# Attention and gated Fourier mixing on one core: keys of one more batch transposed on TensorE, inverse factors loaded from ScalarE's queue, split first loads and last inverse, new order

## The chip, the core and the metric

The kernel runs on one core of a Trainium2 chip. TensorE (PE) multiplies matrices from SBUF into PSUM, VectorE (DVE), ScalarE (ACT) and GpSimd (POOL) work element by element, and 16 DMA engines move data for the queues of SyncE (SP), ACT and POOL. The metric is device time in microseconds (us); a comparison takes the median over several runs.

## The reference

Eight batches, eight heads, 576 positions, head dimension 64, 32 packed queries `p` per head. The output has 576 x 512 values of float32 per batch.

```python
def sm_attn(qq, kk, vv):                 # softmax(scale * q k^T) v
    ...
p_packed = sm_attn(p, k, v)              # 32 packed rows per head
out = sm_attn(q, p_packed, p_packed)     # every position looks at the packed rows
x = out with heads side by side          # 576 x 512
proj = x @ w_proj                        # 576 x 1536
x1, x2, x3 = three parts of proj
x2_conv = irfft(rfft(x2) * rfft(filter_fft))     # along the 576 positions
y = x1 * x2_conv * x3
return y @ w_out
```

## The kernel before

Each batch passes four stages, which the source writes as generators and interleaves over neighbouring batches (`together`, line 1088): `front(b)` does both attentions, `turn(b)` the projection and the forward transform, `middle(b)` the product with the filter's spectrum and the gates x1 * x3, `back(b)` the inverse transform and the output projection.

*Loads.* `load(b)` (line 622) brings k, v and q of a batch as tiles kn, vn, qn (float32 in memory, float16 in SBUF) through POOL's queue, two buffers each. Lines 638 to 654 start the filter, the forward factors wc and wt, the weights wp in three parts, the inverse factors ac (line 652, POOL's queue, four planes of 576 columns: three factors, and a fourth plane that holds negated values of the first two) and wout. POOL's queue has up to eight loads under way; the next one waits for a landing.

*front(b).* The keys are needed with head dimension on the partitions. `k_turn(g)` (line 729) transposes two heads on PE, six products of 96 columns into PSUM (tile kTp), copied to SBUF (tile kT, a ring of five) by DVE or ACT in turn; four such groups make a batch. For the batches in `KEYS` (line 606: 6 and 7) four DMA transposes on SP's queue do it (line 770). `q_turn` (line 750) does the same for q, or one DMA transpose per batch for those in `TURNED`. Then come `score1` (tile s_b), the exponential e, the product with v (pv), its division (rz, ppn), a transpose into ppk, the second scores `score2` (s_b, s2t_b), their exponentials, sums zs, reciprocals zr and the normalised weights a2n.

*turn(b).* Products qp with wp, copied to qm by ACT; products fp and fpt with the forward factors, copied by ACT (ez, fa) and combined (fa); a2n transposed to a2t, on PE or, in batches 5 to 7 (`FLIP`), by one DMA transpose on SP's queue.

*middle(b).* `spectrum(m)` makes f on PE, DVE multiplies it with the filter (tt; the tile h3 or "h" is the filter's spectrum, made at the start from the products hp), POOL adds (gm). `gate` makes x1 and x3 on PE (shown as x_b), ACT copies x1 (x1s), DVE multiplies (w).

*back(b).* `inverse(m)` (line 1033) multiplies gm with ac, for one block m of 128 channels over the first 512 columns: for batches other than 0 three products over 288 columns (even positions) and three over 224. Batch 0 (`APART`) uses another set of five products and is the only one that reads ac's fourth plane. DVE multiplies the result with w into y. A last call covers the remaining 64 columns of all four blocks (into yt). `project_out(n)` (line 1048) multiplies 128 columns of y of all four blocks with wout (tile o_b), copies to os and stores. For the last batch it works in two halves of 256 columns, one copied by ACT and one by DVE; the last call (n = 4) stores each half by itself, half the rows from SP's queue and half from ACT's.

*Order.* The generators don't set the final order. A recorder (class `Recorder`, line 221; in the profile all its instructions have line 538) notes every operation, and a planner (`schedule`, line 316) walks through time with costs for each operation and queue. Among the operations that are ready on an engine it takes the one with the lowest number in a table `PRIORITY` written into the source (line 86, a packed string with one entry for each operation). The instructions go out in that order, each engine's own. Where PE would have nothing in the first 34 us, the planner inserts filler products on zeros ("spin", lines 382 and 1129).

Of the kernel before, what the change touches and what calls it, by code (L numbers as in the profile page):

```python
# [19 lines left out]
P = 128  # L20
# [23 lines left out]
def _constants(S):  # L44
# [37 lines left out]
    ac = _f16(np.stack([*inv, np.where(COLUMN_T % 2 == 0, -inv[1], -inv[0])]).transpose(1, 0, 2))  # L82
# [4 lines left out]
    'c-oy-2RxN+8$ZuEMoLCSBqSoqmKCxq$1Ege%gPMN-Xmm0_RP)}iYVE#3W<sc8S$z&Q8?%MoPE&y`@Z+Po-^*}y6@}0{@1*3f587`q5+rudu2{1'  # L87
    '8~O8>?SK{W-z*%YoO~+%Tt%^qQ}W9U2RlaHGHLgJl$x5MTjnE|O=tXmbA`*LWsEs{+0(W2u5F=3<VZLF^xH>q4MinR3hA+#L$2=GUWVuNsrK=('
    'P?H64>q|+UKWnSXPlIHbwCnrUz3>H84Ekhorn#g_O|LykA@SxMO{a^7*i8=VRcVk5*jOEYF{Kve?CYLpb+yu2k?}gE`7^}VDcHP&v97D5g`1Jl'
    'HEm@FTSaqAEn`Dfc?Ctdq@<PvTu??*l}}Av@dCfvWmOFsEir*WO#@9axr_5UHlexow*(;f!h!>W+@!#fy-Gg%<0>f!!z{!}=7*d=(+Z4h(%UJo'  # L90
    '1TNEt^!E4kcSm<u29r?H{vsVCg}{_5XU9kHd;8=)3!dKd?TsHpO;mJ}-=kiV2Qlrj5)3!lHcNDm(BJka+r#_m*3fK8M)K@??|{Z9D#BE3G|<R>'
    '%%f|w91psiJ1H~9PFyxYn(CGmXt+7v&Gqx>Dy=VbwfWc=InKss!X#>GYohugqqXPdGFxMBRX;a3Gl{e?Z8syMtXl<>Xm#&#2iaA{KIB?iN&P}Y'
    '2B>YGW3OY{__V93Vf1IqY;D!E)|y|nl^r#GovrhgS=o(Eh2M%d8^0D8RW`jIO!)phCg(|AW{22}s`#DS53W<u&si4!Iy`LJ5<WnAejrF@;^)ET'
    'Z^x+)uJkW`9-gCsY_!NhzW)-8W^ftkQC5@sfym|ASN_RbM5ShAVCc;Tm4qCeRa$A|Qlulh5u4U23ukAtysU!svdrAH+*)KQWzA~!JioZMu!Sv;'
    'xrPPbpikFy!MpL%=h^M$)P_YlR!OFa^w5I9+Jvszg{Go`+2QwUoy(VKtWMbkSO(f8I)vE?Ojgw~Oi)p4ULc)*9r;DIac1`E(pXBAi=YCx)SOmG'
    'VysK>QUTr65Z&gF<!WvP0T#8j10&UoZ9fB2$djY{Y8qaa2-;09NlL$G`t(%sOO<rv<445^_mP1IHtMm#ul^bdoA%%k);%k|k4&DCU0jV_L4aFa'
    '_88Mqj#C0Bj*5#Mq2}j2%5(Z83zhKxgF<vHM-H7v0_^NG^ibwwl)zDFX*UJu!5;6dCF^7s1LN_%dTZ*+qAAx*`6vrRr8hDM!@|n>Ha?OMjZl+w'
    'P``zOXVv{#J}(Y#-lqP1{cCNQl@@(_jH$f2M*~ld*vAO}g!o%RXJ^LWjP?%q4ZrGZ>1*z4?s}nn?*#Y8rgCCl*2kZo9HPfs%7$vX>kZxsEN&W&'
    'Q?j0*=KR6c_;jSTx!_CGapO;RX*a5Frq~tU4+j9)*c$(yv!d;^)U=>%b65dW&h&Goj<nzk{<VGUo8D~$&CeevL8Cn?e4RaXzb8c&+`3_SQ%KX_'
    'wYIf8ZUTl_Kx!^MnH`w@{B3by#PEv4>>g6n&~RUmxZBsSy109}`iC0F_yt(`>gan$7}(r0Ft}@B?eDJPA*XNcaL32T-PXzN7mb^-tg5NlxpaXB'  # L100
    'dq-;@E0e=sj>?@S$#ta%>f4jD((=6DnQY`}`yCKZyzNuusV>39-jrKxP*T+QxY(gF!a6U*qqO>#T>mA<dvHBd7Dakt87a6P$FRPQ<29G6yEK`}'
    'hdXnt>-s;o-Eg?yDyA!GB%;f&$KcH9$ml|EIXUtG;w^RSteVG#R5^AoeFuK|3r6O9^+j)97IL?WjRKt{FH;|&<Dg)BtpJyiInTFr$5=n&Q966+'
    '^zT%aIn_zJ*Wy#UG0!R{2HJflD4iZh<;IXPbuw#D$w22MoNb;ewsg<bl$OJJM8nd(UaJdhsziuANDI&7FayeqUe>>k>S!6u;Nsa&i~O?w8TQxU'
    '%%_2tbcxFd7&Q!B|3yK~%*{YWx%W7X`Y87y%Bj<&fA1HeAZJ{lUt-+9J~lr|GR=GdgwpTRhp5ShU*g}G<X`MQl3%jfnpd@v?^jh8pYXco5?hfD'
    'MO<dEUHRsd)~LW_lhW|;3VV@R0n0a4x#cfXJL=k>S2nsO6qi?~*EbYBRF{0(o!4Urx6{&q-@X;<;cLvqB0y`Q=X+iHE~%MiW@MasSM}4xzs|=~'
    '96GjdfL3(Au47=bYpnmX#*gyO{4=RVVTlgPretd?C8R~0*@!YkBwxBj)R{Pb#8o*rJ`vV+VKVKDkpWPxpFg<fp`<IU@0qA*znfirXr)=G827lS'
    'xNXv#oBN`M^tCW4N!=@Y1xb3Ie$Jbr%Pt?>R(!hqMn`Mj&knXCm)2Gw$s0D7ju}c(9}oUMZxmoTT;I~wQW2KZ)jseo#6pw@M#5?;4-W~n_?>JY'
    'a63NBD99)EO=^8(_>B7~-|>}&!P%MOg1oaz%Emfeib`@9^$aB>IYgMX*{+*i(L5!~by-M8#++S6LHU5XxPU6>6}n3|s8#suLm4=ILNtbc3PI^t'
    'PZq|#7z+5AU*xG{yc`-*QyKK|FLEKz6tUy{ha|Zq5Bmir#7D`_P9?4lri84B-Vdutj7<=BDe$^y?W$tTMMkT3-A&d^!v9_jh3YY*JMo`%wN>QV'
    'IXh)!4>_OUmXV+zT72?_YV7xq!#XdXv=-FLBRgaN=7-4Ixmx=~O-ZM=oS5VBk&TnOz^fyhELC(VO5Y)KSW|5Cllmgd+SP_@!ptm3g-(}7D|xf$'  # L110
    'r$)^Kqsg9|qsz)yB`kQkR3qWyE;fTT=|780U#&E=(I~Rn#rv-Zw)W2Ve*Vz)PFVAC{bH|ILF!H8t4tzK!b&sB%3ZUA?1Q4cGD<4rQtt$Y=al;8'
    'hZyQ7+o;+{)kJs)KhAE*4twx2`bI|T{i)|QJu8d-tL=3HhiSjCE2tPbR`ELcTKmcB>#N@Kf@@o<b(s233r2psU)DeQYsDZ$0HFU4BVAyiI{B*J'
    '$lhvI>^Sot9&s}Z-76h#H_4#6f!6U!eK)Q&)#k(XjCn6=$nQU8c+S`RQPr85^)|;nE&-uoRpHr2QNC4t2jM0i6ZP&d?w`|Pd2cRoTFB;nTjB7i'
    '-@>Cb$2PaXr`egE6Q2Xsyw54a*#&1h7wP*|V~@q~q(}v~D>o?RD%J?{aOqSf?R!aitjI~?9{J)pIpX^(=2GZ7E2K<PK*B)P(py<w%g|F?%It=P'
    'wSl#nx=yFdg3Kx-D{X38ep_w$!jWHOqhu7DX%we*nAl#jOrEJ#?jTc<vk!dm1}<`NZEs6NbaX^?N@7e<erAwYV_E*A`*kfrg-?s@{i^H}no{Bu'
    '{gT})b9_^?eV;$ePs;PGr=-ZQdh!C%zlUwVpbDP`%PBblH99Rdg>ylU?Uj$;zb;a+S2C1V(lLX3I@!KmBlpSip1V6S`{KjNM-g>y8JcI5_d;vC'
    ')**9Ig=w+Rvbx?3_A&G~jz1a-`c~po7!@q>ab|vEkY-`A;=H1atelIZm1k4Ivu6XHZ{M~ilAg+$q^DtB-FHQtU6A`c&-{KVjbCDxfn75V!+p=v'
    '`nn4TD?+-PU$gw~%qnj$INIJ6?&DTu;U5zbnwwSERv6WCg|Sr=k&y00Q{3C07t>na&{$AkU7l-KsaO%5<J9#rH{0A)(BtNfu%Vv*rir&bjbF>F'
    'R(>O$DdKIjlB!>(KlaY8;lF2_<C1WrBD%uMNI?700TK9Q`QVc_zU7*M>l+pM*)avNArWh1+}}si?<Kldmj>T@R#N$Jo#LY2#Q>MPUVM39S2C#S'
    'n%}JXe@Ly1%`Se(?*2QGcWz?pZfr!0_KBRb%-ICNW{=yR8h#=tC||VlpE<Qx=E`yN9t(S+OrNdPiYO4Hk$}q~=*0G1fO;9*<m45uN<ZW{;6iJf'  # L120
    'rWJ5E2*Kx}AH#cIL&F3vmTh67u6)ldDNg<EVz{BTYl@oX8*5Gnb;X!m87Fs*e0M!l&zBn^7o_4G+23}LaF?x9@vHCU)VUw+<>NQ)VM{{)MT%+i'
    'oNx%Q6H~ZHYP?HpaG0AL!=1vAiT#HJuJf8qomJ#lP~l!ee5XZ%i^K7{{<obyv*2n95;oo0z4Cm=IrIgOt4Uj!*;#ve+1;tls7LfxR}I_gM*EMn'
    'J87I)F@HZc`ghMt=f?Qlhriny)wp#jNZWpqpFk#?NT2bx<)+><vqTGgEFYw$qhy(-InB$#dyM1vxubI?u(zH=<F4<f-esI*@0|a&F}YgYmT-i#'
    'mHH_u4J$J%{bA~yl2hM$XNTABF3o^s>CPWIx=3ar>%bC;N5dF^A}ACJKmiP)Mo<*N&|DG#^$$VKKmZ740r~|kffM@Q2#VbVf+hgK?usD@VI69U'
    'n6Pu0A^5KeC5QS&4{-8ZHlp<acqV!Qh+ai3iD3~T!pZ<d*szA-yn&k`5Qt_10EonFhL!?}O~g3}>s<h^2|I%uV7MsRZ9YQ&OTyX&U_c=OjG-99'
    '=)y2iYe3W(l?13a6c4&(#&+Oat6*D+g0d4uM2bMv4^e0#1P4LD9Z@C@HenNt>mWqVA(jS+!~r}Y^bm%MAc#f}*+Y)A7m61kgqWP17zpBjpiQDN'
    '6oJ}>jGUYdpS{E|K_mhJqN0sahMvVJBw)vf8^BcGme}SFLT!maZ31pH0|d6!2i7qF6bB9yND%KZkSKF7J8iGE9YMjM#Hhs=6cXHp?!OU$ts#8H'
    '5rPL`9e{Eah}aGX*a>L|I=s;U674lyBK*O5P~!C3k#P_t1lP)N^+db^iFt@ZitZqoet}sEC2AOuKczJ;HAzT_S*SGHg10-lHnD?E^!z4{g;9n}'
    'CX`0hejv7SZ9NF&4)vrYs1*c){s|q3SxN9INMMs-_#mMxg6Q@SC3NwPjg58mgC+ENg6nZ0s?gBl0EE!lfIpZ1)(3&aJODuCQli`jcS-+)w^0Ox'
    '5d%m3OTujl;u8-BLs^fhClG?%6>r!U5jSJ#wv&VyBWfL?yl`oS`{HB(C~SAGZ_9rW@()cEyCFf2ki9sy0HHkoZU5WurX7bZN(q9Phi)1O$ktf^'  # L130
    '!k|bbF1bK-6W(6i=!8K#2nym_CgIS9U@jxO)M2I|m|nlNWY-k{z#sk)e63*r&}9kYgNzFT1pGrU#G^r?njpbGOqQXYw~2WGfY2?G$p6=+f6z_v'
    'D83xgurYX`03I0X@P+IM0*--y!DZ3*2x9XF%SU3qyKY_pwizIiyRTdz{<Z~y{OLZnt&?t7jl&1oUWUY$BXP@jqXIx&euIC|4Z+O<#0~&3_ZrCd'
    'n*m64Y7%!J92VpbgE4$0^3SFbEdlYJgUE0Ye?D(Ri%m-+Wf0<<Dc1G><WCTHvxV&N6J%F#@NdL6qqB%m$~ypqf6|Jnd~AVj(SHDhSUi3'
# [3 lines left out]
class Op:  # L137
# [43 lines left out]
    def hold(self):  # L181

        if self.engine == "POOL":
            return 780
        return 1000 + 0.45 * self.packets() if self.what == "dma_start_transpose" else 440
# [7 lines left out]
    def transfer_ns(self):  # L193

        far = self.ins[0] if self.reads == [] else self.out
        piece, size = far.shape[-1] * mybir.dt.size(far.dtype), far.size() * mybir.dt.size(far.dtype)
        self.piece_ns = max(piece / 25.2, 16) if piece > 1000 or self.engine == "POOL" else max(piece / 21.5, 17)
        if self.reads and self.engine != "POOL" and piece > 1000:
            self.piece_ns = piece / 18
        if self.what == "dma_start_transpose":  # L200
            piece, size, self.piece_ns = 256, self.out.size() * 2, 20
        return size / piece * self.piece_ns / 16
# [18 lines left out]
class Recorder:  # L221
# [3 lines left out]
    SLOW = 6000.0  # L225
# [90 lines left out]
    def schedule(self):  # L316
# [18 lines left out]
        def live():  # L335

            heads = [q[0] for q in queues.values() if q]
            beside = 31 if len(heads) > 1 else 0
            total = sum(max(x[1].piece_ns, beside if x[1].what == "dma_start_transpose" else 0) for x in heads) * (1.6 if moved[0] < self.SLOW else 1.0)
            return [(x, x[1].piece_ns / total) for x in heads]  # L340
# [82 lines left out]
        def issue(e, t):  # L423
            while free[e] <= t + 1e-6:
# [19 lines left out]
                if op.dma():  # L444
                    took = op.hold()
                    begins = t + (2760 if e == "POOL" else 950)
                    opens[e] = max(opens.get(e, 5900 if e == "POOL" else 0), begins)
# [43 lines left out]
        while events:  # L491
# [20 lines left out]
            elif what == "moved" and x == turn[0]:  # L512
                advance(t)
                for e, q in queues.items():
                    if q and q[0][0] <= 0.02:
                        op = q.pop(0)[1]
                        at(t + (1500 if e == "POOL" else 600), "done", op)
# [27 lines left out]
def kernel(  # L545
# [23 lines left out]
    NI = ac_np.shape[1]  # L569
# [19 lines left out]
    ac = const.tile([P, NI, S], FP16, tag="ac", name="ac")  # L589
# [16 lines left out]
    TURNED, KEYS, NK = (4, 5, 6, 7), (6, 7), 5  # L606
# [562 lines left out]
```

## Time and profile before

| what | value |
|---|---|
| median of 5 runs | 189.47 us (188.94 to 196.76) |
| the profiled execution | 189.87 us |
| its span in the profile | 188.1 us |
| DVE, ACT, POOL busy | 143.1, 123.5, 137.6 us |
| landings of kn, vn, qn of batch 0 | 12.46, 15.29, 17.95 us |
| landings of wp's three parts | 22.26, 24.43, 27.16 us |
| landings of kn, vn, qn of batch 1 | 30.18, 33.42, 36.16 us |
| ac: issued, landed, first used | 24.71, 38.30, 38.81 us |
| last product on PE ends | 182.8 us |
| last store lands | 186.73 us |

Times are counted from the start of the span. An engine's busy time is the union of its instructions; a product on PE is counted from its start to its modelled end, and products overlap, so the distance between two starts is what one costs. The granted clock of PE was 0.99 of full over the span. Loads are counted in bytes written.

### The profile page before, as it was taken

How to read it: one execution, taken by the hardware profiler on the slowest of the kernel's cores; microseconds unless marked ns; L12 is line 12 of the kernel's file. 1: busy time of each engine (PE TensorE's matmuls, PEld its weight loads, DVE VectorE, ACT ScalarE, POOL GpSimd, SP SyncE). 2: the span in 40 equal slices, each digit the busy share in tenths (PEclk: the TensorE clock that was granted, in tenths of full speed). 3: DMA queues.
4: the chain of work that ended last, by engine and by line, in shares of the span. 5: the costliest groups of instructions: out<-in, count | busy, mean ns of one | idle time of the engine just before them, and what ended most of it. 6: DMA issues, size and time to landing. Idle time of an engine off the chain costs nothing.

```text
span 188.1 us, 5930 instructions
## 1 busy us (share of the span) xinstructions
PE 175.8 (93%) x2477; PEld 117.4 (62%) x2477; DVE 143.1 (76%) x268; ACT 123.5 (66%) x261; POOL 137.6 (73%) x111
## 2 busy tenths in 40 slices
PE   0999879999999999999999999999999999999980
PEld 0447645668656767666567556757767578566770
DVE  7266899978478889987899779979757876797550
ACT  2357548698779998596964698368688843623440
POOL 7532447973898599898967998599299979979300
PEclk9999999999999999999999999999999999999996
DMA  5999999999999999999999998998772370151374
GB/s 141 288 203 197 204 202 199 265 197 203 194 218 252 200 215 191 142 194 192 187 173 237 193 165 143 167 145 243 134 210 71 112 122 3 42 181 59 127 267 112
DMA packets 52715, 32.86 MB, mean 175 GB/s; under 512 B 24592, under 2 KB 47760, under 8 KB 52688
## 3 DMA queue, kind: packets, MB, share of 16 engines
q0 software_dynamic: 29456, 17.11, 65.0%
q1 hardware_dynamic: 22576, 14.59, 37.0%
q10 hardware_dynamic: 656, 0.79, 1.6%
q8 instruction: 19, 0.31, 0.7%
q14 instruction: 8, 0.07, 0.1%
HBM read 35.39 MB, written 9.44 MB: 238 GB/s over the span
## 4 chain that ended last, share of the span: by engine, by line
PE 80%; DMA 5%; POOL 5%; ACT 3%; DVE 3%; issue 1%; DVEq 0%
PE x_b L538 28%; PE o_b L538 15%; PE f_b L538 8%; PE hp L538 5%; PE fp_b L538 5%; PE s_b L538 5%; PE qp_b L538 3%; PE kTp_b L538 3%; PE pv_b L538 3%; DMA w<-in_moe_filter_fft_dram 3%; POOL gm L538 3%; DMA a2t<-a2n 2%; PE qTp_b L538 2%; PE fpt_b L538 1%; POOL a2n L538 1%; PE a2tp_b L538 1%
## 5 line engine op out<-in xcount | busy, mean ns | idle before, releaser
L538 PE MATMUL x_b<-a2t,qm 128*128 128x64 f16 (+3 forms) x400 | 45.7, 243 | 0.2 <-DMA a2t<-a2n 0.2
L538 POOL TENSOR_TENSOR tt<-tt,tt 128x1024 f32<-128x1024 f32 x14 | 33.2, 2369 | 13.5 <-DVE tt L538 13.5
L538 DVE TENSOR_TENSOR tt<-f_b,h 128x1024 f32<-128x1024 f32 x32 | 38.5, 1220 | 4.2 <-PE f_b L538 3.0
L538 POOL TENSOR_TENSOR gm<-tt,tt 128x512 f16<-128x512 f32 (+1 forms) x30 | 39.6, 1348 | 0.8 <-DVE tt L538 0.3
L538 PE MATMUL x_b<-ac,gm 128*128 128x64 f16 (+3 forms) x300 | 39.0, 249 | 0.0
L538 PE MATMUL o_b<-wout,y 128*128 128x512 f16 (+1 forms) x144 | 35.4, 356 | 0.0
L538 ACT COPY x1s<-x_b 128x512 f32<-128x512 f32 (+1 forms) x40 | 21.9, 548 | 14.1 <-PE x_b L538 7.5
L538 PEld LDWEIGHTS <-qm 128*128 128x128 f16 x400 | 25.1, 98 | 9.7 <-issue 1.1
L538 ACT ACTIVATE os<-o_b 128x512 f32<-128x512 f32 (+1 forms) x36 | 20.4, 570 | 15.5 <-PE o_b L538 15.0
L538 DVE SCALAR_TENSOR_TENSOR y<-w,x_b 128x512 f16<-128x512 f32 x32 | 21.2, 683 | 9.0 <-PE x_b L538 8.7
L538 ACT CAST qm<-qp_b 128x512 f16<-128x512 f32 x48 | 26.1, 608 | 2.6 <-PE qp_b L538 2.4
L538 DVE TENSOR_TENSOR w<-x1s,x_b 128x512 f32<-128x512 f32 (+1 forms) x40 | 24.5, 628 | 2.9 <-PE x_b L538 1.9
L538 ACT ACTIVATE e<-s_b 96x384 f16<-96x384 f32 (+1 forms) x48 | 23.2, 525 | 5.3 <-PE s_b L538 5.1
L538 PEld LDWEIGHTS <-gm 128*128 128x128 f16 x300 | 22.3, 98 | 6.2 <-POOL gm L538 0.8
L538 PE MATMUL f_b<-qm,fa 128*128 128x512 f16 x80 | 24.7, 380 | 0.1
L538 POOL TENSOR_TENSOR fa<-ez 128x512 f16<-128x512 f32 x15 | 19.0, 1279 | 2.7 <-ACT ez L538 2.7
L538 PEld LDWEIGHTS <-a2n 128*128 128x128 f16 x210 | 14.0, 98 | 6.9 <-DVE a2n L538 1.7
L538 PEld LDWEIGHTS <-y 128*128 128x128 f16 x144 | 13.0, 98 | 7.1 <-issue 0.4
L538 POOL TENSOR_TENSOR a2n<-e,zr 128x1152 f16<-128x1152 f16 x7 | 15.0, 2136 | 1.2 <-DVE zr L538 1.2
L538 DVE TENSOR_REDUCE zs<-e 128x36 f32<-128x1152 f16 (+2 forms) x10 | 11.0, 1108 | 1.7 <-ACT e L538 1.7
L538 ACT COPY ez<-fp_b 128x512 f32<-128x512 f32 x16 | 9.2, 588 | 3.6 <-PE fp_b L538 3.2
L538 PE MATMUL fp_b<-wc,a2n 128*128 128x256 f16 x64 | 11.1, 273 | 0.0
(82 smaller groups left out, 276.6 us busy)
## 6 DMA issues: line engine op xcount, KB each, us to landing
out_dram<-os SPq DMA_DIRECT2D x24, 256.0 KB, 2.8
kn<-in_k_dram POOLq DMA_DIRECT2D x8, 576.0 KB, 14.1
vn<-in_v_dram POOLq DMA_DIRECT2D x8, 576.0 KB, 13.2
qn<-in_q_dram POOLq DMA_DIRECT2D x8, 512.0 KB, 13.9
out_dram<-os SPq DMA_DIRECT2D x14, 128.0 KB, 2.4
wp<-in_moe_w_proj_dram POOLq DMA_DIRECT2D x3, 512.0 KB, 16.5
out_dram<-os SPq DMA_DIRECT2D x17, 64.0 KB, 2.0
w<-in_moe_filter_fft_dram SPq DMA_DIRECT2D x2, 512.0 KB, 6.4
```

Of the source, the lines that this page charges most:

```text
L538: ins = op.call(*op.args, **op.kw).ins
```

## The change

- `KEYS` loses batch 6: its keys are transposed on PE by `k_turn`, 24 products and four copies, instead of four DMA transposes on SP's queue. Batch 7 keeps its DMA transposes.
- ac's fourth plane is no longer loaded. Three planes come from ACT's queue instead of POOL's. The issue stands in `turn(0)`, behind a copy of one element that ties it to the copy of fpt into fa; ACT makes the fourth plane by two negations of 288 columns, which need the loaded planes.
- kn and qn of batch 0 are loaded in two halves of four heads each.
- The inverse of the last batch runs over two blocks m and 256 columns at a time instead of one block and 512 columns. Its second half spans columns 256 to 512, so it has products of 32 and of 224 columns.
- The last store of the last batch (n = 4) is no longer cut into column halves: two stores instead of four.
- The planner's costs change (a DMA issue 520 instead of 440 ns, slower same-type loads on POOL's queue, later start and completion of transfers on SP's and ACT's queues, contention 1.7 instead of 1.6 until 5.5 instead of 6.0 us), and `PRIORITY` is replaced, so that the order of all engines and of the loads may differ everywhere.

```diff
-    ac = _f16(np.stack([*inv, np.where(COLUMN_T % 2 == 0, -inv[1], -inv[0])]).transpose(1, 0, 2))
+    ac = _f16(inv.transpose(1, 0, 2))
...
-        return 1000 + 0.45 * self.packets() if self.what == "dma_start_transpose" else 440
+        return 1000 + 0.45 * self.packets() if self.what == "dma_start_transpose" else 520
...
+        if self.engine == "POOL" and self.ins[0].dtype == self.out.dtype:
+            self.piece_ns *= 1.65
...
-    TURNED, KEYS, NK = (4, 5, 6, 7), (6, 7), 5
+    TURNED, KEYS, NK = (4, 5, 6, 7), (7,), 5
...
-        nc.gpsimd.dma_start(kn[:], k[b].rearrange("h (p i) d -> p h (i d)", i=KI))
+        for h in (slice(0, 4), slice(4, 8)) if b in (0,) else (slice(0, 8),):
+            nc.gpsimd.dma_start(kn[:, h, :], k[b, h].rearrange("h (p i) d -> p h (i d)", i=KI))
         nc.gpsimd.dma_start(vn[:], v[b].rearrange("h (p i) d -> p h (i d)", i=KI))
-        nc.gpsimd.dma_start(qn[:], q[b, :, 0:512, :].rearrange("h (p i) d -> p h (i d)", i=4))
+        for h in (slice(0, 4), slice(4, 8)) if b in (0,) else (slice(0, 8),):
+            nc.gpsimd.dma_start(qn[:, h, :], q[b, h, 0:512, :].rearrange("h (p i) d -> p h (i d)", i=4))
...
-    nc.gpsimd.dma_start(ac.rearrange("p i s -> p (i s)"), d_ac.ap()[:].rearrange("p i s -> p (i s)"))
...
+        if b == 0:
+
+            nc.scalar.copy(out=ac[0:1, 0, 0:1], in_=fa[0:1, 0, 512:513])
+            nc.scalar.dma_start(ac[:, 0:3, :].rearrange("p i s -> p (i s)"), d_ac.ap()[:].rearrange("p i s -> p (i s)"))
+            for e, c in enumerate((slice(0, EVEN), slice(EVEN, S))):
+                nc.scalar.mul(out=ac[:, 3, c], in_=ac[:, 1 - e, c], mul=-1.0)
...
-        def inverse(*ms):
-
-            cols = slice(0, MAIN) if len(ms) == 1 else slice(MAIN, S)
+        def inverse(*ms, cols=None):
+
+            cols = cols or (slice(0, MAIN) if len(ms) == 1 else slice(MAIN, S))
...
+            if len(ms) == 1:
+                nc.vector.scalar_tensor_tensor(out=y[:, ms[0], cols], in0=w[:, ms[0], cols], scalar=SC_Y, in1=x2[:, 0, :],
+                                               op0=ALU.mult, op1=ALU.mult)
+            else:
+                to = y[:, ms[0]:ms[-1] + 1, cols] if cols.stop <= MAIN else yt[:, :, x, :]
+                nc.vector.scalar_tensor_tensor(out=to, in0=w[:, ms[0]:ms[-1] + 1, cols], scalar=SC_Y, in1=x2[:],
+                                               op0=ALU.mult, op1=ALU.mult)
...
-                    for c in range(split):
-                        c = ts(c, DM // split)
-                        (nc.sync, second)[u].dma_start(rows[64:128, 3, c], os_[64 * u:64 * u + 64, c])
+                    (nc.sync, second)[u].dma_start(rows[64:128, 3, :], os_[64 * u:64 * u + 64, :])
 
         for m in range(ND):
-            inverse(m)
+            if b == B - 1:
+                inverse(m % 2 * 2, m % 2 * 2 + 1, cols=slice(m // 2 * 256, m // 2 * 256 + 256))
+            else:
+                inverse(m)
```

The products inside `inverse` come from the same `terms` as before, cut at the given columns.

## The prediction

> **What bounds the kernel now.** I read the page first (busy shares, slices), then busy time by stretch, then the chain of waits at both ends, then the DMA issues one by one (all issue and landing times below).
>
> ```profile
> span 188.1 us, 5930 instructions
> ...
> PE 175.8 (93%) x2477; PEld 117.4 (62%) x2477; DVE 143.1 (76%) x268; ACT 123.5 (66%) x261; POOL 137.6 (73%) x111
> ...
> PE   0999879999999999999999999999999999999980
> ...
> DMA  5999999999999999999999998998772370151374
> ```
>
> The reader is to see two full resources. PE is full from the 7th slice to the 38th; the DMA engines are at 80% or more to the 28th, about 132 us. The stretches say which of them counts (columns: stretch, its length, then busy us of PE, PEld, DVE, ACT, POOL with counts, granted clock, DMA share, GB/s):
>
> ```profile
> 15.00:20.00 5.00, 4.63 (x117) 3.36 (x114) 3.14 (x8) 3.26 (x7) 2.55 (x4) 1.00 1.42 198
> 20.00:25.00 5.00, 4.05 (x60) 2.74 (x57) 4.14 (x12) 3.92 (x8) 1.43 (x3) 1.00 1.29 204
> 25.00:30.00 5.00, 4.25 (x52) 2.49 (x53) 4.33 (x11) 2.85 (x7) 2.93 (x4) 1.00 1.40 199
> 30.00:35.00 5.00, 5.00 (x73) 3.40 (x72) 5.00 (x8) 4.42 (x10) 4.42 (x5) 1.00 1.36 240
> ...
> 100.00:110.00 10.00, 10.00 (x176) 6.50 (x181) 8.30 (x19) 5.92 (x14) 9.02 (x7) 1.00 1.37 200
> ...
> 180.00:188.10 8.10, 2.80 (x33) 2.26 (x30) 1.82 (x5) 1.54 (x4) 0.00 (x0) 0.80 0.57 183
> ```
>
> From 30 to 180 us PE is idle for 0.34 us in all (0.07 in 50 to 60, 0.09 in 70 to 80, 0.01 in 110 to 120, 0.17 in 150 to 160). So the late transfers cost nothing there, and whatever is added to PE in that stretch is paid in full. What can be won lies at the ends. Between 15 and 30 us PE is idle for 0.37 + 0.95 + 0.75 = 2.07 us, and 2.79 us of its busy time are the filler products "spin" (rows of 0.72, 0.38, 0.71, 0.38 and 0.60 us): 4.9 us without useful work. The chain of waits shows why:
>
> ```profile
> 18.08 1.29 DVE h L538 x2
> 19.37 0.09 DVE rz L538
> ...
> 20.27 0.46 PE qTp_b L538 x8
> ...
> 20.75 1.01 ACT qT L538
> ...
> 21.79 0.27 ACT ppk L538
> ```
>
> Two steps of batch 0 stand in the wrong order. The products of pv end at 18.8, but the reciprocal waits for two h products on DVE until 19.3 (0.5 us). The second ppk copy could follow the first at 20.35 and stands behind the copy of qT on ACT until 21.79 (1.0 us after the qT copy began).
>
> **The change part by part.** Durations are from the profiled execution.
>
> *Keys of batch 6 on PE.* Added: 24 transposes, two copies on ACT and two on DVE.
>
> ```profile
> 14.57 1.19 PE L538 MATMUL kTp_b<-wc,kn 96*128 96x96 f16 x24
> ...
> 90.78 2.80 SPq L538 DMA_TRANSPOSE kT<-kn  x2
> ...
> 100.96 3.30 SPq L538 DMA_TRANSPOSE kT<-kn  x2
> ```
>
> One transpose takes 0.206 us from start to end, but 24 take 1.19, so they start (1.19 - 0.21)/23 = 0.043 us apart: 24 x 0.043 = 1.02 us of PE, on the path. The copies (2 x 0.66 on ACT, 2 x 0.44 on DVE) lie beside PE: between 100 and 110 us ACT has 4.1 us free and DVE 1.7. Without that cover they would cost up to 2.2 us. Removed: four issues that hold SP's queue for 6.1 us; qT of batch 6 (issued at 105.94) and a2t of batch 5 (115.03) stand behind them. PE never ran dry for those, so they give 0 to 0.34 us back, and I take 0. Term: +1.0.
> The Trainium skill (TensorE: Matmul & The Clock Gate, "Part 4: PE-mode transpose") speaks against this part: it gives about 275 ns for a transpose in a kernel. By that, 24 would cost 6.6 us and the sum below would become a loss of some 4 us; the row of 0.043 us between starts decides.
>
> *Inverse factors on ACT's queue.* POOL's queue loses ac, which landed at 38.30, 2.14 us after qn of batch 1 (36.16); three quarters of it, 1.6 us of the same engines, come back from ACT, so loads behind it come 0.5 us earlier: nothing, since PE is full there. ACT gets a one-element copy (nearest row 0.26), an issue (0.38 to 0.55 in its rows) and two negations of 128x288 (between the rows of 0.375 for 256 and 0.59 for 512 columns: 0.8 together), 1.5 us in all, hidden in 30 to 40 us, where ACT is busy 7.6 of 10. The new wait is the first negation's, for the landing. Behind it on ACT stand the x1s copies of batch 0 and the e and kT copies of batch 1; DVE (w) and PE (score, pv) wait for those. The nearest rows for the landing are the SP stores of 64 to 256 KB between 50 and 80 us beside a full POOL queue, 5.1 to 7.0 us from issue; with 1.6 more for the size, 6.7 to 8.6. Issued after the copy of fpt (27.41 + 0.37), so at 28 or a little earlier, it lands at 35 to 37. The first product with ac stood at 38.81. I take 0; the bounds are -0.3 (less in POOL's queue) and +4 (the negation placed near 32 and the landing at 36).
> The Trainium skill (DMA: Bandwidth & Descriptors, "Issuing engines are not separate DMA queues") says that transfers started by ACT, SP or POOL share the same 16 engines and interleave. By that, vn and qn of batch 1 land 1.6 us later (33.42 to 35.0, 36.16 to 37.8), just at their uses (36.08, 37.73), and the sum would be up to 1 us worse; no row of this trace shows two loads side by side.
>
> *First loads in halves, and the order of the start.* Two more POOL issues (0.79, 0.89) lie in time when POOL does nothing else. The ninth load waits for a landing (pn of batch 1 was issued at 10.55, after 10.27); now wp is that ninth. The queue still moves qn until 17.95, so no hole opens; without that cover wp would land about 1 us after 22.26. The first half of kn can land 1.1 us sooner (half of 12.46 - 10.27), that of qn 1.3 (half of 17.95 - 15.29). With both misplaced steps put right (0.5 + 1.0) and some 0.9 of the halves, batch 0's chain moves up by 2.4 us. What fills the time is middle(0): for each m 0.22 x 6 = 1.3 us of PE beside 1.22 + 0.68 = 1.9 us of DVE (tt, w), PE dense to 0.68. That makes 1.6; with hp products pushed into the remaining holes I take -1.8. Bounds: 0 (wp landings at 22.26, 24.43 and 27.16 and kn of batch 1 at 30.18 hold everything back) and -3.3 (two thirds of the 4.9).
>
> *Last inverse in halves.* Products of 256 columns start 0.109 us apart, of 64 columns 0.029, of one column 0.025. On that line (0.417 ns a column) 288 cost 0.122 and 224 cost 0.096. Before, one m takes 3 x 0.122 + 3 x 0.096 = 0.654; now 3 x 0.109 + 3 x 0.026 (32 columns) + 3 x 0.096 = 0.693. Times four: +0.16. DVE's four y stay as wide.
>
> *Last store whole.* SP's last issues start at 182.86, 183.42, 184.07 and 184.83, the last landing is at 186.73, and the span ends 1.36 later; ACT's three (below) run beside.
>
> ```profile
> 182.88 1.64 ACTq L538 DMA_DIRECT2D out_dram<-os  x3
> ```
>
> One issue less on each queue: -0.65. Bounds 0 and -0.9.
>
> **Sum:** 1.0 + 0 - 1.8 + 0.16 - 0.65 = -1.3 us. The profiled execution took 189.87 (span 188.1 and 1.8 around it); it becomes 188.6, span 186.8. The median is 0.4 below that execution, so 189.47 - 1.3 = 188.2. The order elsewhere is costed at nothing: PE has no idle time for it to remove.
>
> **Rivals.**
> *Slower: ACT waits for ac.* One mechanism: ACT works in order and the first negation comes before the landing. For it: landings of 5 to 7 us beside POOL's queue; between 30 and 35 us ACT has 0.6 us free in 5. Against it: a margin of 2 to 4 us before 38.81. Each us held adds a us: a hold of 1.3 eats the gain, and from 1.9 on the kernel is slower by more than 0.57. At 2.5 us: 190.7.
> *The loads set the start anyway.* wp and kn of batch 1 come no sooner; the head gives nothing: 189.47 + 1.16 - 0.65 = 190.0, within what can be told apart. Against it: the two misplaced steps are no loads.
> *The start closes much further.* The head gives 3.3: 186.7. For it: hp, f and x products wait in store while spin runs. Against it: DVE is busy 8.5 of 10 us from 20 to 30.
> *The halves are not used* (both issued together, last stores in the old place): 188.2 + 0.65 = 188.85.
>
> **How the numbers follow.** About 0.3% (0.57 us) is what a measurement here can tell from no change. Forecast 0.45 (187.3 to 188.9, a little of it inside 0.3%), far closing start 0.18, loads rule 0.13, ACT held 0.20, halves unused 0.04. Faster: 0.43 + 0.18 + 0.01 = 0.62. Same: 0.02 + 0.09 + 0.03 = 0.14. Slower: 0.20 + 0.04 (loads rule with a short hold of ACT) = 0.24. Range 186.2 (half a us beyond the far closing start) to 190.7 (a hold of 2.5 us).
>
> **What would show it.** PE with 24 more kTp and 12 more short products between 30 and 183 and still no idle time: right. Spin fewer than 25 and the first a2n product before 23.6: the head gained. An ACT wait for the ac landing above 1.9 us, or kn of batch 1 landing after 31: wrong. Last PE product to end of span below 5.3 us: the tail gained.

## The result, and the profile after

The changed kernel takes 190.19 us (median; 189.58 to 190.88), the kernel before 189.76 beside it: a ratio of 1.002, 95% interval 1.0011 to 1.0029. The forecast was 188.2, faster. The time lies in the forecast's range, but on the other side of no change, by about +0.4 us. The profiled execution took 189.76 us, its span 188.0.

First the page of the changed kernel (all lines as on the page of the kernel before):

```profile
span 188.0 us, 5990 instructions
...
PE 177.1 (94%) x2515; PEld 118.6 (63%) x2515; DVE 144.1 (77%) x270; ACT 123.7 (66%) x266; POOL 138.3 (74%) x112
...
PE   0999889999999999999999999999999999999990
...
DMA  5999999999999999998499999997532542134545
```

PE has 1.3 us more to do in the same span. The stretches, with the columns of before:

```profile
15.00:20.00 5.00, 4.98 (x103) 3.46 (x98) 3.75 (x9) 2.77 (x8) 3.23 (x5) 1.00 1.41 199
20.00:25.00 5.00, 4.08 (x49) 2.22 (x49) 4.69 (x13) 3.25 (x6) 1.95 (x3) 1.00 1.25 205
25.00:30.00 5.00, 4.69 (x47) 2.41 (x48) 3.96 (x8) 3.47 (x8) 2.53 (x3) 1.00 1.40 199
30.00:35.00 5.00, 4.73 (x61) 3.08 (x60) 4.92 (x9) 4.11 (x9) 4.99 (x5) 1.00 1.34 242
...
100.00:110.00 10.00, 10.00 (x152) 6.41 (x150) 8.15 (x18) 5.68 (x13) 9.92 (x7) 1.00 1.37 211
```

From 15 to 30 us PE is idle for 1.25 us instead of 2.07. From 30 to 35, where it had no idle time, it now has 0.27. The chain of waits at the start shows that the two misplaced steps were put right:

```profile
18.23 0.69 DVE h L541
...
18.93 0.22 DVE ppk L541
...
19.42 0.70 DVE qT L541
...
20.17 0.41 PE s_b L541 x8
```

One h product instead of two stands in front, and the qT copy went to DVE. The first a2n product starts at 22.08 us (23.6 before). Behind 30 us the chain of the kernel before runs over PE alone until 50; its pieces between 30.75 and 33.2 us are

```profile
30.75 1.35 PE x_b L538 x8
32.10 0.81 PE kTp_b L538 x19
32.91 0.08 PE qTtp_b L538
32.99 0.22 PE kTp_b L538 x5
```

That of the changed kernel does not:

```profile
31.29 0.26 ACT pk L541
31.55 1.07 ACT kT L541 x2
32.64 0.26 ACT pk L541
32.93 0.59 ACT x1s L541
33.56 0.41 PE kTp_b L541 x6
```

PE sends the turned keys and an x1 product to ScalarE and has to wait for its copies before it can go on (the transposes at 33.56 need the PSUM buffer that x1s gives back). In 30 to 50 us 3.75 us of the chain are ScalarE's, in 50 to 70 another 5.6 (2.4 before).

To see where the time went, I counted what PE had done at a given time: each product's columns at 2.4 columns per ns (the prediction's 0.417 ns a column), at least 25 ns a product, fillers left out, from the starts in the trace. Products that use only 32 columns of the array count a quarter (pv) or an eighth (qp), as four or eight of them run side by side: their starts stand some 4 ns apart.

| PE's work done by (us) | 30 | 50 | 70 | 100 | 130 | 160 | all |
|---|---|---|---|---|---|---|---|
| before | 15.13 | 33.60 | 51.23 | 78.82 | 106.41 | 134.03 | 156.11 |
| after | 16.57 | 33.92 | 51.28 | 79.29 | 106.55 | 134.61 | 157.21 |
| lead | 1.44 | 0.32 | 0.05 | 0.47 | 0.14 | 0.58 | |

The count jumps by whole products of 0.2 us: the lead is 0.80 at 28 us, 1.44 at 30, 1.23 at 32 and 0.80 at 34. It is gone at 70. At 160 us a lead of 1.02 would only pay for the 24 transposes, and 0.58 is there. The end is shorter: from the last product's end to the end of the span 4.52 us instead of 5.29.

The start itself varies. In eleven profiles with the old start, the same product at 12 us stands between 0.88 us earlier and 0.38 later than in the profile of before (mean 0.25 earlier); in seven with the new one, between 0.17 earlier and 0.67 later than in the profile of after (mean 0.27 later). In this pair both draws favour the new order, by 0.52 together, so the 1.44 would be some 0.9 on average. The same count, averaged over the five profiles of each order that keep it to 70 us (before, e1, e3, e17, e18; after, e2, e7, e11, e15), gives a lead of 0.75 us at 30 us, 0.05 at 50 and -0.2 at 70. Both figures are estimates; the loss behind 30 us is in both.

### The profile page after: what moved, and what is told of

It reads as the page before. It is cut to its first block, busy times and chain, and to the rows that moved or that the text cites. A ratio compares the mean times of both kernels' runs of the same rounds, so it can differ in the third digit from the quotient of the medians.

```text
span 188.0 us, 5990 instructions
## 1 busy us (share of the span) xinstructions
PE 177.1 (94%) x2515; PEld 118.6 (63%) x2515; DVE 144.1 (77%) x270; ACT 123.7 (66%) x266; POOL 138.3 (74%) x112
## 3 DMA queue, kind: packets, MB, share of 16 engines
q10 hardware_dynamic: 720, 1.23, 2.1%
## 4 chain that ended last, share of the span: by engine, by line
PE 83%; ACT 6%; DVE 6%; POOL 1%; issue 1%
PE x_b L541 28%; PE o_b L541 16%; PE f_b L541 9%; PE fp_b L541 5%; PE s_b L541 5%; PE hp L541 4%; PE kTp_b L541 4%; PE pv_b L541 3%; PE qp_b L541 2%; ACT qm L541 2%; DVE zs L541 2%; PE qTp_b L541 2%; ACT e L541 1%; PE spin L541 1%; PE a2tp_b L541 1%; PE fpt_b L541 1%
## 5 line engine op out<-in xcount | busy, mean ns | idle before, releaser
L541 PE MATMUL x_b<-a2t,qm 128*128 128x64 f16 (+3 forms) x400 | 48.0, 243 | 0.1
L541 PE MATMUL x_b<-ac,gm 128*128 128x288 f16 (+5 forms) x312 | 36.8, 246 | 0.0
L541 PE MATMUL o_b<-wout,y 128*128 128x512 f16 (+1 forms) x144 | 36.1, 355 | 0.0
L541 PEld LDWEIGHTS <-qm 128*128 128x128 f16 x400 | 25.8, 98 | 8.9 <-issue 1.2
L541 ACT ACTIVATE e<-s_b 96x384 f16<-96x384 f32 (+1 forms) x48 | 23.8, 526 | 4.9 <-PE s_b L541 4.4
L541 ACT CAST qm<-qp_b 128x512 f16<-128x512 f32 x48 | 25.6, 602 | 2.0 <-PE qp_b L541 1.9
L541 PEld LDWEIGHTS <-kn 96*128 96x128 f16 x168 | 10.3, 97 | 5.0 <-issue 0.9
L541 PE MATMUL kTp_b<-wc,kn 96*128 96x96 f16 x168 | 12.8, 206 | 0.2 <-ACT x1s L541 0.2
```

The costliest lines, as they stand in the source:

```text
L541: ins = op.call(*op.args, **op.kw).ins
```

## The experiments

In most of them every engine keeps its order: the planner sees the old instructions, and a table (`nc.instead`) replaces single ones when they are emitted; the diffs are cut to what is emitted. Then equal products can be matched, and their starts compared with the profile of before (or after). This table (us, median of the products behind each time) is the main instrument; a step between two columns is what was lost or won there (e18 has another order from 168 us on). It is one profile of each kernel; the medians of many runs, given with each experiment, have intervals of 0.25 to 0.55 us to either side.

| kernel, against before | 20 | 34 | 45 | 55 | 120 | 150 | 182 |
|---|---|---|---|---|---|---|---|
| e1 keys alone | +0.01 | +0.01 | +0.01 | +0.02 | +0.98 | +0.86 | +0.59 |
| e5 ac alone | -0.25 | +0.42 | +0.42 | +0.41 | +0.43 | +0.43 | +0.62 |
| e8 fewer products | -0.47 | -0.69 | -0.78 | -0.78 | -0.78 | -0.78 | -0.67 |
| e9 more products | -0.37 | +0.39 | +0.61 | +0.60 | +0.62 | +0.63 | +0.50 |
| e10 more VectorE | -0.32 | +0.69 | +0.75 | +0.75 | +0.75 | +0.75 | +0.60 |
| e13 less of both | +0.39 | +0.16 | +0.17 | +0.22 | +0.22 | +0.21 | +0.29 |
| e14 less VectorE | -0.20 | -0.20 | -0.20 | -0.17 | -0.18 | -0.18 | -0.51 |
| e18 end alone | -0.88 | -0.88 | -0.38 | +0.09 | +0.05 | +0.05 | |
| **against after** | | | | | | | |
| e7 whole loads | +0.32 | +0.33 | +0.33 | +0.34 | +0.35 | +0.35 | +0.40 |
| e11 ac from SP | +0.45 | +0.45 | +0.45 | +0.46 | +0.47 | +0.47 | +0.47 |
| e12 more products | -0.17 | +0.91 | +0.91 | +0.91 | +0.92 | +0.97 | +0.98 |
| e15 less VectorE | +0.27 | +0.26 | +0.26 | +0.27 | +0.27 | +0.26 | +0.28 |
| e16 less of both | +0.67 | +0.08 | +0.09 | +0.09 | +0.09 | +0.08 | +0.29 |

### The parts one by one

**e1: the keys alone**, in the old order.

```diff
-    TURNED, KEYS, NK = (4, 5, 6, 7), (6, 7), 5
+    TURNED, KEYS, NK = (4, 5, 6, 7), (7,), 5
```

> The kernel before, with one part of the change: keys of batch 6 transposed on PE. The order is that of before; the 24 transposes and four copies stand 2.5 us ahead of their first scores. Theory A (PE is full from 30 to 183 us, so what is added there is paid in full): 24 x 0.043 = +1.0 us, ratio 1.0054, last PE product 1.0 us later. Rival (SP's queue and the DMA engines, freed of four transposes, give something back): at most +0.4 us, ratio under 1.002.

Measured: ratio 1.001 (0.9994 to 1.0025). The products behind the transposes start 0.98 us later, 24 x 0.041: the size of one is right. But 0.12 are back at 140 us and another 0.35 at 160. There the chain of waits of the kernel before runs beside PE:

```profile
143.50 4.92 POOL gm L538 x4
148.41 2.10 POOL a2n L538
150.52 4.19 DMA a2t<-a2n
```

It ends with a landing at 154.71 us; in e1 the same landing is at 154.82, although PE is 0.86 late. PE, which waited for it before, comes later and waits less. (Profiles with the old keys differ by -0.33 to +0.18 at this place, so some of the 0.35 is chance.)

**e2: the change without its keys**: the four DMA transposes of batch 6 put back on SP's queue, issued from 98.9 us on, as its kn lands at 98.8 in the new order (90.7 in the old).

```diff
-    TURNED, KEYS, NK = (4, 5, 6, 7), (7,), 5
+    TURNED, KEYS, NK = (4, 5, 6, 7), (6, 7), 5
```

> The changed kernel with that one part undone: keys of batch 6 come by four DMA transposes again, issued from 99.5 us on, all else in the changed kernel's order. Theory A (paid in full): 1.0 us faster than the changed kernel, so about 189.2 and a ratio to before of 0.997. Rival (the changed order was laid out for PE transposes, and the DMA transposes come back into SP's queue ahead of qT and a2t): no faster than the changed kernel, ratio 1.002 or more.

Measured: 194.8 us, ratio 1.0267 (1.0238 to 1.0295). The waits of PE in e2 (us in total, times, longest):

```profile
PE s_b L523 <- DMA kT<-kn: 4.4, 1, 4.4
```

The new order leaves no time for these DMA transposes; this says nothing on an order made for them.

**e3 and e18: the end alone**: the last inverse in halves, the last store whole, the changed kernel's order from 168 us on, all else as before. **e17: the store alone**, order kept.

```diff
-                    for c in range(split):
-                        c = ts(c, DM // split)
-                        (nc.sync, second)[u].dma_start(rows[64:128, 3, c], os_[64 * u:64 * u + 64, c])
+                    (nc.sync, second)[u].dma_start(rows[64:128, 3, :], os_[64 * u:64 * u + 64, :])
```

> The kernel before, with the last inverse in halves and the last store whole; from 168 us on the order is the changed kernel's, before that it is that of before. Theory A: +0.16 for 12 more short products and -0.65 for one store less at the end, -0.5 us, ratio 0.9974, and the time from the last PE product to the end of the span falls from 5.3 to 4.6. Rival (the end is set by the last landing, not by issues): 0, ratio 1.000, still 5.3.

> The kernel before, order kept, only the last block's rows stored whole and not in two column halves (two issues fewer, one on SP's and one on ScalarE's queue; the whole one stands where the second half's stood). The forecast's term: -0.65 us, ratio 0.9965, seen as the distance from TensorE's last product to the end of the span, 5.57 us before to about 4.9. If the landing of the last transfers and not their issues sets the end: 0 to -0.15 us.

> The kernel of e3 once more (the kernel before, with the last inverse in halves, the last store whole and the changed kernel's order from 168 us on), as the candidate that beats both kernels, now with more rounds. The forecast's terms for the end: +0.16 - 0.65 = -0.49 us, ratio 0.9974. If the gain that e3's profile showed was only its earlier start: ratio 0.999 to 1.000.

Measured: e3 ratio 0.9985 (0.9956 to 1.0014), which is no verdict; e18, the same kernel in more rounds, 0.9973 (0.9949 to 0.9997), 189.24 us; e17 0.9972 (0.9949 to 0.9994), 189.27 us. The store alone gives the whole 0.5 us; what the halves cost or gain is too small for these runs, whose intervals are +-0.45 us. From the last product to the end of the span e17 and e18 take 4.67 and 4.52 us; nine profiles with the old store lie between 4.61 and 5.34 (mean 5.08), eleven with the new one between 4.03 and 5.27 (mean 4.60), so a single profile does not show the gain. By their medians these two kernels beat both others.

**e5: the inverse factors alone** on ScalarE's queue, in the old order.

```diff
-    nc.gpsimd.dma_start(ac.rearrange("p i s -> p (i s)"), d_ac.ap()[:].rearrange("p i s -> p (i s)"))
...
+            nc.scalar.copy(out=ac[0:1, 0, 0:1], in_=fa[0:1, 0, 512:513])
+            nc.scalar.dma_start(ac[:, 0:3, :], d_ac.ap()[:, 0:3, :])
```

> The kernel before with every engine's order kept, and only the inverse factors moved from POOL's queue to ScalarE's (one-element copy, load, two negations in ScalarE's idle time before the ppk copy of 37.73 us). The batch-2 keys behind them on POOL's queue should land some 2.1 us earlier (40.88 to about 38.8). The forecast (cost nothing): ratio 1.000, within 0.002. Theory C (loads set the pace from 30 to 70 us, so a lead is lost whatever the order): earlier loads are a gain, 0.5 to 1.5 us, ratio 0.992 to 0.997. Theory B (ScalarE and the new order set it): loads are no help and ScalarE has 1.39 us more to do, 0 to +0.6 us, ratio 1.000 to 1.003.

Measured: ratio 1.0012 (0.9996 to 1.0029). kn and qn of batch 2 landed 1.1 us earlier (39.75, 42.90) and the starts behind them did not move: PE does not wait for those two. But 0.67 us were lost in one wait, from 28.49 to 29.25 us (f behind f, 763 ns instead of 97): I had put the copy and the issue ahead of the ez copies, and PE waits for the fa that VectorE makes from these. In the changed kernel they stand behind the qm copies. **e11** tells what they cost there: the same factors, whole, from SP's queue, order kept (**e6**, meant to do this, gave the planner another shape of load; it laid out another order from 40 us on, and the kernel took 210 us).

```diff
-            nc.scalar.dma_start(ac[:, 0:3, :].rearrange("p i s -> p (i s)"), d_ac.ap()[:].rearrange("p i s -> p (i s)"))
-            for e, c in enumerate((slice(0, EVEN), slice(EVEN, S))):
-                nc.scalar.mul(out=ac[:, 3, c], in_=ac[:, 1 - e, c], mul=-1.0)
+            nc.sync.dma_start(ac.rearrange("p i s -> p (i s)"), d_ac.ap()[:].rearrange("p i s -> p (i s)"))
```

> The changed kernel with its order kept, but the inverse factors loaded on SP's queue, all four planes, no negations: ScalarE is rid of the issue (0.33 us at 29.34) and of two negations (2 x 0.436 at 36.0); the one-element copy stays. Against the changed kernel (190.2): theory B (the chain of waits of the changed kernel runs over ScalarE for 3.75 us between 30 and 50, where before it is all TensorE) expects 0.4 to 1.0 us less, 189.2 to 189.8. Theory C (loads) expects no gain, 190.0 to 190.4, or a small loss, as the transfer has 33% more bytes.

> What e6 was meant to be: the changed kernel with every engine's order kept, the inverse factors loaded whole (four planes) on SP's queue, the issue (0.33 us) and the two negations (2 x 0.436 us) taken off ScalarE. If ScalarE's share of the change is what loses the lead between 30 and 70 us: -0.5 to -0.9 us against the changed kernel, 189.3 to 189.7, the products from 40 us on starting that much earlier. Theory D (VectorE sets the pace there): -0.3 to +0.1, 189.9 to 190.3.

Measured, e11: 190.35 us, ratio to before 1.0025 (1.0012 to 1.0037), the changed kernel's own time; the starts keep their +0.45 from 20 us to the end. The factors on ScalarE cost nothing there that these runs can tell (+-0.25 us). What e11 takes from ScalarE lies at 29.3 us (0.33) and 36.0 (two negations of 0.44).

**e7: the changed kernel with whole first loads**, order kept.

```diff
-        for h in (slice(0, 4), slice(4, 8)) if b in (0,) else (slice(0, 8),):
+        for h in (slice(0, 8),):
```

> The changed kernel with its order kept, but first keys and queries of batch 0 loaded whole, as before: the first half of the keys is there 1.3 us later (11.14 to about 12.4). The forecast's price (time gained at the start is kept to the end): +0.9 to +1.3 us against the changed kernel, 191.1 to 191.5. If the lead is lost again by 70 us whatever (theories B and C): 0 to +0.4, 190.2 to 190.6, with the count of products done at 30 us 0.5 to 1.3 us lower and that at 70 us the same.

Measured: 190.41 us, ratio 1.0037 (1.002 to 1.0054). The keys came whole at 12.39 us instead of half at 11.14. Its products at 12 us stand 0.32 later than after's, those of the other profiles with halves 0.27 on average: the halves gain next to nothing, 0.2 us by the medians and 0.3 by the ratios, within the +-0.3 of each ratio. The lead at 30 us is the order's.

**e4: the start alone**: the diff's parts for the loads, ac and the planner's costs, with entries of `PRIORITY` that give the new order until 30 us and then the old one; `KEYS`, the last inverse and the last store as before.

```diff
-    TURNED, KEYS, NK = (4, 5, 6, 7), (7,), 5
+    TURNED, KEYS, NK = (4, 5, 6, 7), (6, 7), 5
```

> The kernel before, with split first loads and ac from ACT's queue (three planes, fourth by negation), and the changed kernel's order for what that kernel does in its first 30 us; after that the order is that of before, as far as readiness lets it. Keys of batch 6 by DMA, end as before. In the changed kernel PE had 1.4 us more useful work done by 30 us and had lost it again by 70 us. Theory B (lost because of the new order between 30 and 70 us): with the old order there it is kept, -1.4 us, ratio 0.9925. Theory C (from 30 to 70 us loads and the other engines set PE's pace, and any lead is lost): 0, ratio 0.998 to 1.002, with PE's waits between 30 and 70 us above those of before by about 1 us.

Measured: 195.4 us (six runs, 191.32 to 198.43; the profile is of one of 194.86). It loses nearly 5 us of PE's work between 100 and 160 us, where the old order follows on a sequence of loads that it was not made for, so the total says little. But its first 70 us count: PE's work done at 30 us is 16.14, 1.0 ahead of before; at 50 us it is 33.28, 0.3 behind. The gaps of PE (as measured below) between 30 and 50 us add up to 1.47 us instead of 0.27, and 3.9 us of its chain there are VectorE's. The lead is lost in the old order too, in this one profile.

### What takes the lead

**e8 and e9**: in the old order, the second product of each of the five pairs of batch 0's spectrum (28 to 33 us) left out, or the first one done twice.

```diff
             for t in range(2):
-                nc.tensor.matmul(f[:], fa[:, t, ts(m, P)], qm[:, t, ts(1, DM)], start=(t == 0), stop=(t == 1))
+                nc.tensor.matmul(f[:], fa[:, t, ts(m, P)], qm[:, t, ts(1, DM)], start=(t == 0), stop=(t == 1 or b == 0))
+                if b == 0 and t == 1:
+                    nc.instead[nc.ops[-1]] = []
```

> The kernel before with its order kept, but the second product of each of the five pairs of batch 0's spectrum left out (five products of 512 columns, 5 x 0.213 = 1.07 us of TensorE between 28 and 33 us; batch 0's output is then not the reference's). A lead of 1.07 us made early, with no other change. The forecast's picture (TensorE full, so time taken off it is kept): -1.0 us, ratio 0.995. Theory C (loads pace 30 to 70 us): the lead is lost, ratio 0.999 to 1.000. Theory B (the lead was lost only by the new order): -0.7 to -1.07, ratio 0.9945 to 0.9965.

> The kernel before with its order kept, and the first product of each of the five pairs of batch 0's spectrum done twice (+5 x 0.213 = 1.07 us of TensorE between 28 and 33 us, nothing else). Theory D (from 18 to 40 us VectorE has almost no idle time and sets the pace, so TensorE has slack there that its rows do not show): 0 to +0.5 us, ratio 1.000 to 1.0025. The forecast's picture (TensorE full, every product paid): +1.07 us, ratio 1.0055.

Measured: e8 ratio 1.0009 (0.9991 to 1.0027), e9 1.0035 (1.0022 to 1.0048). By the starts, 1.07 us more of PE cost 0.98, and 1.07 us less gave 0.31 (from -0.47 to -0.78). By the medians the one cost 0.7 (0.4 to 0.9), the other gave nothing (+0.2, -0.2 to +0.5). The rest went into waits that were shorter or not there before. They are read from the gaps between PE's starts, beyond 2.4 columns per ns, wide products only (here and below, in ns):

```
                                          before    e8   e13
f behind f             28 us (qm, fa)         97   325   324
x_b behind x_b         30 us (qm)            <40   183   183
s_b                    33 to 34 us (kT)      <40   189   187
x_b<-ac                38 us (ac, gm)         36   242    36
```

In brackets is what the waiting products read and other engines write. By the releasers in the trace the first wait of e8 ends with VectorE's copy into fa (28.31 us), the second with ScalarE's copy into qm (29.81), the third with ScalarE's copy into kT (33.20). The four grew by 0.81 us together. For the last one the chain of waits of e8 names POOL:

```profile
35.72 2.37 POOL gm L540
...
38.16 0.59 PE x_b L540 x2
```

But in e3 the same product starts 0.23 us before that gm ends, so it does not need it. It starts 0.13 us behind ac's landing (38.03), as it does in e14 and e18 (0.14, 0.14): the releaser is a load on POOL's queue, and the view named the engine that ended nearby.

**e10 and e14**: one tt multiplication of that row done twice, or one left out (POOL's sum then adds the first part twice). **e13**: left out together with the products of e8. The diff is e10's; the others have `m == 2` and an empty list.

```diff
             nc.vector.tensor_tensor(out=x[:], in0=f[:].unsqueeze(1).broadcast_to([P, 2, DM]), in1=h, op=ALU.mult)
+            if b == 0 and m == 0:
+                nc.instead[nc.ops[-1]] = [nc.ops[-1]] * 2
```

> The kernel before with its order kept, and one multiplication tt<-f_b,h of batch 0 on VectorE done twice (+1.22 us of VectorE at 31 us, none on TensorE). Theory D: paid almost in full, +0.7 to +1.2 us, ratio 1.0035 to 1.0065. The forecast's picture (TensorE sets the pace and VectorE has idle time beside it): 0 to +0.3 us, ratio 1.000 to 1.0015.

> The kernel before, order kept, with only the multiplication of e13 left out (-1.22 us of VectorE). Theory D: TensorE's own path, the longer one by 0.3 us, stays: 0 to -0.15 us. If VectorE alone sets the pace from 18 to 40 us: -0.7 to -1.2 us.

> The kernel before, order kept, with both paths of batch 0's spectrum shortened: the five products left out as in e8 (-1.07 us of TensorE) and the multiplication tt<-f_b,h of the third part left out (-1.22 us of VectorE; the sum that read it adds the first part twice; batch 0's output is then not the reference's). In e8 the chain of waits left TensorE for VectorE and POOL (fa, gm, tt, w, kT, qTm, tt, then gm on POOL), which ended 0.3 us before TensorE's own path. Theory D (two paths end at the same time, so one alone can't be shortened with profit): -0.85 to -1.07 us, seen as products from 45 us on that much earlier than those of 20 us. If something else holds TensorE there (ScalarE's copies, loads): -0.3 us as in e8.

Measured: e10 ratio 1.0023 (1.0008 to 1.0037), which is +0.4 us (0.2 to 0.7), and +1.07 us by the starts, for 1.22 us of VectorE. e14 0.9984 (0.9965 to 1.0003), 0.00 by the starts from 20 to 45 us. e13 0.9998 (0.9977 to 1.002): -0.39 us at 40 us, -0.17 at 55, with the first three waits of e8 unchanged. So work added to either engine is paid, between 0.4 and 1.1 us of it, and work taken from one, or from both, is hardly given back. My picture of two paths (-0.85 to -1.07) fell too: the waits for fa, qm and the turned keys are round trips from PE to ScalarE or VectorE and back.

A fourth path is POOL's load queue. e18 starts 0.88 early by chance, and loses all of that again at two waits: 0.67 us at 37.9 for ac (0.04 in before; landing at 38.42, product at 38.56), and 0.71 at 53.0 for POOL's fa (0.24 in before). The chain of waits of e18 before the second:

```profile
32.23 17.61 DMA vn<-in_v_dram
...
50.39 0.73 POOL qn L522
...
51.64 0.77 POOL vn L522
...
52.43 1.29 POOL fa L522
```

POOL cannot issue its next loads before vn of batch 2 has landed (49.85 us), and fa stands behind these issues. In e3, which started 0.64 early, ac landed at 37.84 and vn at 48.99 us, and it kept its lead: there the loads were early by chance as well.

**e12, e15 and e16**: the same edits in the changed kernel: five products more; one multiplication less; both less.

> The changed kernel with its order kept, and the same five products of batch 0's spectrum done twice (+1.07 us of TensorE between 27 and 32 us). Theory D: TensorE reaches this stage 0.9 us earlier than before and only waits there, so the products fit in: 0 to +0.4 us against the changed kernel, 190.2 to 190.6. If TensorE's own order and mode switches lose the lead: +1.07 us, 191.2.

> The changed kernel, order kept, with the same multiplication left out (-1.22 us of VectorE at 32 to 36 us). If the lead that the new start gives TensorE (0.9 us at 30 us) is held back by the path over VectorE and POOL: -0.4 to -1.0 us against the changed kernel, from 40 us on. If it is held back by ScalarE's copies of the turned keys at 31 to 33.5 us and TensorE's order: 0 to -0.2 us.

> The changed kernel, order kept, with the five products and the multiplication left out. If VectorE's path alone holds the lead back: as e15 or up to 1.07 us more, -0.9 to -1.9 us. If ScalarE's copies and the order of the key transposes behind them hold it: 0 to -0.4 us, with the waits of TensorE at 31.7 and 33.2 us grown by what was left out.

Measured: e12 191.2 us, ratio 1.0074 (1.005 to 1.0098): +1.08 by the starts, paid in full, and +1.0 against the changed kernel by the medians. e15 1.0045 (1.0027 to 1.0063), -0.01: this multiplication does not hold the changed kernel. e16 1.0013 (0.9995 to 1.0032): -0.59 of 1.07. The waits of PE tell most:

```
                                      after   e11   e12   e15   e16
x_b behind kTp           31.7 us        218   218   240   238   239
kTp for x1s's buffer     33.2 us        384   383   383   382   493
s_b behind x_b           42.5 us        249   249   249   247   247
```

In the trace the first of them ends with a copy of the turned keys by VectorE, the second with ScalarE's x1s (in e16 with a tt of VectorE), the third with ScalarE's third copy into qm. The first, and the chain before the third:

```profile
31.42 0.46 DVE L541 COPY kT<-kTp_b 128x576 f16<-128x576 f16 x1
...
31.93 1.02 PE L541 MATMUL x_b<-a2t,qm 128*128 128x512 f16 x4
```

```profile
41.10 1.57 ACT qm L541 x3
42.67 0.04 issue
42.72 0.22 PE s_b L541 x2
```

In e12 PE comes 0.9 to 1.1 us later at them (against its own start) and the waits stay, so no load sets them. The multiplication that e15 leaves out stood at 30.20 us, earlier than the expectation says, directly ahead of VectorE's copy at 31.42; VectorE then stood idle for 1.12 us until PE's transposes were done, and the wait stayed as long. So these waits come from PE's own products, through a copy on VectorE or ScalarE and back to PE, in the sequence of the new order. The three make 0.85 us. Over 30 to 70 us all gaps of more than 15 ns add up to 1.97 us (0.76 before), and the narrow qp products come in four groups instead of three, 0.3 us more in changes of shape. Together that is 1.5 us, about the 1.4 which the lead of this pair loses. The other gaps (0.18 us at 57.7 behind a tt of VectorE, 0.23 at 58.9 behind POOL's a2n, 0.12 at 68.5 behind ScalarE's ppk, several of 0.06) I only read from the trace; no run touched them.

The sum of the gaps belongs to the sequence and not to the early start: it is 1.93 to 1.98 us in all five profiles with the new order (after, e2, e7, e11, e15), and 1.96 in e12, where PE comes 0.9 to 1.1 us later at them. With the old order it is 0.76 to 0.77 in before, e1, e3 and e17, and 1.67 in e18, which started early.

## Why the prediction was wrong

**Start, -1.8.** Half there: both misplaced steps were put right, the first a2n product came 1.5 us earlier (2.4 predicted), the holes between 15 and 30 us shrank from 2.07 to 1.25 us, the fillers did not (2.83 us instead of 2.79), and PE was 0.75 to 0.9 us ahead at 30 us (1.44 in this pair of profiles). The halves, to which I gave about 0.9 of the chain, gain nothing that e7 could separate from zero.

**"From 30 to 180 us PE is idle for 0.34 us in all", and so "the order elsewhere is costed at nothing: PE has no idle time for it to remove".** This is the step that failed. It takes for granted that PE sets the pace, so that time won before 30 us reaches the end, and that a new order brings no waits of its own. In fact several other paths end within a few tenths of a us of PE's in the same stretch. The new order has gaps of PE of 1.97 us there instead of 0.76 between 30 and 70 us, and 0.3 us more in changes of shape, in every profile of it; that took the lead. The old order did not keep it either: e4 lost 1.3 us between 30 and 50, and e8, e13 and e18 lost most or all of theirs to round trips over ScalarE and VectorE and to POOL's load queue. A full engine makes added work dear (e9, e12); it does not make saved time count (e8: 0.31 us of 1.07 by the starts, none by the medians). My second rival, "the loads set the start anyway", had the right outcome (190.0) in the wrong place: not wp and kn of batch 1 held the start, but what comes behind it.

**"So the late transfers cost nothing there."** True only at PE's usual pace: in e18 two landings took the 0.88 us that it had gained.

**Keys, +1.0.** The size of one transpose is right (0.98 by e1), the net price smaller: +0.2 by the ratio (-0.1 to +0.5), about +0.5 by the starts, as PE meets the a2t landing with less wait. I had the bound of 0.34 back for the removed transposes and took 0. The rule of about 275 ns for a transpose (the Trainium skill, TensorE: Matmul & The Clock Gate, "Part 4: PE-mode transpose") is the duration of one; here one of 96 x 96 lasts 0.206 us from start to end, and in a row each cost 0.041, which is what the sum needs.

**Inverse factors, 0.** Right: issued at 29.34, landed at 35.06 (5.7 us, I had 6.7 to 8.6), negated from 35.99 without a wait, first used at 36.9; e11 finds no price. The Trainium skill (DMA: Bandwidth & Descriptors, "Issuing engines are not separate DMA queues") says that such transfers interleave with POOL's; the trace agrees: qn of batch 1 came 3.75 us behind vn instead of 2.74, landing at 36.35. So the fear that went with it, a landing just at its use, came close but did not come true: PE's first product with that qn starts at 37.74. The prediction's "no row of this trace shows two loads side by side" overlooks the start, where ScalarE's wc (0.75 to 5.65 us) came beside POOL's pn (1.26 to 10.27).

**End, +0.16 - 0.65 = -0.49.** Right in sum: -0.5 by e18 (-1.0 to -0.1), all of it from the store (e17 -0.5).

**The signs I had named.** First a2n product before 23.6: yes (22.08). No ScalarE wait for ac, kn of batch 1 before 31: yes (29.23). End below 5.3: yes (4.52). PE still without idle time behind 30: no (0.27 us from 30 to 35), and there the forecast broke. Fillers fewer than 25: no (27).

The sum as measured, an estimate: start -0.75 to -0.9, 30 to 70 us +0.95 to +1.4, keys and the rest to 160 us +0.5, end -0.5, together +0.2 to +0.5; the medians say +0.4. The gaps of 30 to 70 us are the new sequence's own (e12). Open is whether any order could have kept the lead with this start: no order made for it was tried, and e4's was patched from two.

## What to carry to other kernels

An engine that is busy without a gap is not the only one that sets the pace: before crediting time saved on it, follow the other paths to the points where they meet it, and credit no more than the shortest slack there; charge added work in full, as the safe side (here 0.4 to 1.1 us of 1.07 to 1.22 were paid). When an order is replaced as a whole, cost the order as an edit of its own, in both directions. Edits behind the last meeting point, such as the last stores, keep their gain.

## What the hardware showed that I had not expected

The same instructions in the same order stood up to 1.26 us apart at 12 us from the span's start (-0.88 to +0.38 in eleven profiles), and most then kept that offset to within 0.05 us until 150 us. So a single profile of each kernel can show a lead of a microsecond at the start that neither kernel has; the starts of equal products, not the spans, show where a difference arises.
